# Four column tiles for every dense product, scores that ride along, a compact head layout and a residual on GpSimd, in a two-layer attention and MLP kernel

## Chip, cores, metric

One core of one Trainium2 chip. The metric is the device time of one execution in microseconds (us), median of the runs named; lower is better. Ratios are the mean time of one kernel's fast runs over that of the other's fast runs of the same rounds, so they are not quite the ratio of the medians quoted.

## The reference

Twice in turn: multi-query attention (32 heads of 16, one shared key and value head) and a mixer with an MLP, each on a normalised input, each with a residual. 2048 tokens of 512 features, bf16.

```python
def _A_ref(x, wq, wk, wv, wo):
    q = (x @ wq).reshape(B, S, 32, 16).transpose(0, 2, 1, 3)
    k, v = x @ wk, x @ wv
    p = softmax(einsum("bhqd,bkd->bhqk", q, k) * 16 ** -0.5)
    return einsum("bhqk,bkd->bhqd", p, v)...reshape(B, S, 512) @ wo

def _B_ref(x, w1, w2, w3, w4):
    h = gelu(layernorm(x) @ w1)          # then four quarters shifted by 1, -1, 2, -2 tokens
    x1 = x + shifted(h) @ w2
    return x1 + gelu(layernorm(x1) @ w3) @ w4      # w3: 512 x 1792

x = x + _A(layernorm(x)); x = x + _B(layernorm(x))     # and once more with the same weights
```

## The kernel before

The file contains a greedy planner. Each piece of work is declared with an engine, a priority, what it reads and writes, and a guess of its duration; the planner plays the engines forward in time, takes the best ready piece for each, and then writes out one fixed order for each engine with semaphore waits. Nothing is decided at run time. The order on TensorE distinguishes three shapes of the array: "Q" for scores (four row tiles of 32 rows), "P" for value products (four column tiles of 32 columns) and "F" for full 128 x 128 products. A product of another shape costs a switch.

The work is cut into half-blocks: two heads, 512 queries, 128 keys, 2048 of them in all. Most go to ScalarE (one exponential over 1024 columns); the others go to VectorE as a "pair", which makes exp from integer steps in four instructions.

```python
def declare_unit(self, g):                       # a half-block on ScalarE: two scores, one exponential
    q = op("PE", fpe, ..., pe=("Q", 512, 256, hs), prio=0)
    op("ACT", lambda e: e.activation(self.EA[...], self.PB[:, b0:b0 + 2, :], ACTF.Exp, scale=0.25),
       dur=0.0505 + 1024 / 1200, prio=0)
    ...
def declare_pair(self, g):                       # a half-block on VectorE
    for i in range(2):
        L = Late()                               # takes one of three spare PSUM banks
        op("PE", ..., pe=("Q", 512, 128, (h,)), prio=0.5, take=L)
        op("DVE", lambda e: e.tensor_scalar(out=J[...], in0=self.PB[:, L.bank, :], ...), give=L)
    for k in (1, 2):                             # two shifted copies
        op("DVE", lambda e: e.tensor_scalar(out=self.JK[:, r, :], in0=J, scalar1=float(self.STEPS[k]),
                                            scalar2=None, op0=ALU.add), dur=t_x4(1024), prio=2)
    ...                                          # one value product each for J, JK, JK
def outproj(self, la, tb, prio=4):               # a dense product: full shape
    ... e.matmul(self.PB[:, L.bank, :], lhsT=self.OT[:, b, q:q + 128], rhs=self.WO[:, b, :], ...)
    op("PE", fpe, ..., pe=mm(512, 2))            # mm() says shape "F"
```

`mlp` does the two wide products with W3 and W4 and adds the residual as a ninth product with the identity. A head's 16 rows stand in 32 partitions, half of them zero, so the query and output projections compute twice what they need. Where the planner's own count of TensorE's activity runs short it adds a "filler", a product with zero weights.

The softmax here doesn't subtract the row's maximum and nothing guards it: scores larger than these inputs give would overflow.

Of the kernel before, what the change touches and what calls it, by code (L numbers as in the profile page):

```python
# [26 lines left out]
class Op:  # L27
    __slots__ = ("eng", "emit", "preds", "npend", "succ", "dur", "prio", "seq", "ready", "start",
                 "end", "take", "give", "dma", "out", "pos", "sem", "vc", "side", "placed", "pe", "feeds")


class Plan:
# [7 lines left out]
    DRAIN = {"ACT": 0.15, "DVE": 0.085, "POOL": 0.1}  # L40
    SELF = 0.035
    MARGIN = 0.2
# [5 lines left out]
    CREDIT = 0.3  # L48
    URGENT = 0.4
    FORCE = 0.6  # L50
    CAP = 1.0
    WAITING = 12.0
    BUNCH = 2
    ALONE = 11
    PATIENCE = 3.0
    SLACK = 0
    NEAR_FILL = 0.2

    def __init__(self, nc, pool_banks):
        self.nc = nc  # L60
        self.res = {}
        self.ops = []
        self.now = 0.0
        self.free_at = {e: 0.0 for e in ENGINES}
        self.heap = {e: [] for e in ENGINES}
        self.order = {e: [] for e in ENGINES}
        self.events = [0.0]
        self.pool = [(0.0, b) for b in pool_banks]
        self.pool_last = {}
        self.left = 0  # L70
        self.dma_free = 0.0
        self.pe_kind = None
        self.pe_end = 0.0
        self.lane = [0.0] * 4
        self.window = 0
        self.activity = [0.0]
        self.warm = False
        self.release = 0.0
        self.pace = None
        self.filler = None  # L80
        self.debt = 0.0
        self.debt_at = 0.0
        self.base = 10.0
        self.units = []

    def op(self, eng, emit, reads=(), writes=(), dur=0.1, prio=None, take=None, give=None,
           dma=0, out=False, side=True, pe=None):
# [3 lines left out]
        o.pe = pe  # L91
        o.feeds = None
# [28 lines left out]
        if self.pace is not None and side:  # L121
            if pe is not None:
                self.release += pe[1] * self.pace / 2400.0
            o.ready = max(o.ready, self.release)
# [51 lines left out]
    def _pick(self, eng, t, dense=False):  # L176
# [6 lines left out]
        pressing = joins and any(o.prio == 0 and o.ready <= t + 1e-9 for o in h) and self.pe_kind != "Q"  # L183
        best = None
        bank = None
        for o in h:
# [11 lines left out]
            key = (low.get(o, o.prio), o.seq)  # L198
            if best is not None and key > best[0]:
                continue  # L200
# [65 lines left out]

    def lend(self, banks, o):
# [9 lines left out]
    def _place(self, o, t):  # L277
# [5 lines left out]
        if o.dma:  # L283
            s = max(t + 1.6, self.dma_free)
            o.end = s + o.dma / 330e3 + 0.6
            self.dma_free = s + o.dma / 330e3
            self.free_at[o.eng] = t + 0.06
# [21 lines left out]
        else:  # L309
            self.free_at[o.eng] = t + o.dur  # L310
            o.end = t + o.dur + self.DRAIN[o.eng]
        heapq.heappush(self.events, self.free_at[o.eng])
        if o.give is not None:
# [3 lines left out]
            heapq.heappush(self.events, o.end + self.MARGIN)  # L317
        for s in o.succ:
# [42 lines left out]
    def emit(self):  # L361
# [6 lines left out]
        nd = 0  # L368
        for o in todo:
            kn = known[o.eng]  # L370
            cand = []
# [19 lines left out]
            if o.dma:  # L391
                nd += 1
                key = f"d{nd}"
                sems[key] = nc.alloc_semaphore(key)
                o.sem = (key, 16)
# [13 lines left out]
        def body(eng):  # L409
            def f(e):  # L410
                for waits, emit, sem, inc in code[eng]:
                    for k, v in waits:
                        e.wait_ge(sems[k], v)
                    emit(e).then_inc(sem, inc)
# [28 lines left out]

EPS = 1e-5
# [3 lines left out]
class Kernel:  # L448
# [13 lines left out]
    STEPS = (0, 43, 85)  # L462
    PARTS = (0.3203125, 0.25390625, 0.2021484375)
# [3 lines left out]
    AHEAD = 7  # L467
    MAX_PAIRS = 2
    BACKLOG = 4
# [24 lines left out]
    def memory(self):  # L494
# [13 lines left out]
        self.WO = sb("WO", [8, 512])  # L508
# [8 lines left out]
        self.OT = sb("OT", [8, 512])  # L517
# [14 lines left out]
        self.SM = sb("SM", [5, 16], dt.float32)  # L532
# [12 lines left out]
        self.SPILL += [(qt[:, i * 512:(i + 1) * 512], [("QT", p, 2 * i), ("QT", p, 2 * i + 1)]) for i in range(4)]  # L545

# [20 lines left out]
    def build(self):  # L567
        with contextlib.ExitStack() as self.stack:
# [3 lines left out]
            self.pl.filler = self.filler if self.FILL else None  # L572
            self.pl.run(self.pump)
            self.pl.emit()

    def head(self):
# [42 lines left out]
        for j in range(3):  # L619
            fill("POOL", self.VD[:, j, :, :, 16:17], self.PARTS[j], vd, 0.2, -7)  # L620
        for c in range(4):
# [3 lines left out]
            if c == 0:  # L625
                self.qproj(0, 0, prio=-6, blocks=(0,))
            if c == 2:
                self.qproj(0, 0, prio=-5, blocks=range(1, 8))
# [5 lines left out]
        fill("POOL", self.WO, 0.0, [("WO",)], 3.5, 3)  # L634
        fill("POOL", self.GP[:, 0, :, 0:2], 0.0, [("GPL", 0)], 0.1, 3)
        wo4 = ins["A_wo"].rearrange("(b g d) n -> g d b n", b=8, g=4, d=16)
        for g in range(4):
            load(self.WO[32 * g:32 * g + 16, :, :], wo4[g], [("WO",)], 131072, 5)
# [15 lines left out]
    def rstd(self, tiles, prio, both=False):  # L654
# [4 lines left out]
        s0, s1, s2, s3, s4 = (self.SM[:, i, a:b] for i in range(5))  # L659
# [10 lines left out]
        root(s0, mv, s4, tg("MV"), tg("R1"), tg("S4"))  # L670
        if both:
# [4 lines left out]
            root(s3, s2, s4, tg("S2"), tg("R2"), tg("S4"))  # L676

# [24 lines left out]
    def ln_in(self, la, tiles, prio=None):  # L702
# [6 lines left out]
        for tb in tiles:  # L709
            op("DVE", lambda e, tb=tb: e.tensor_scalar(  # L710
                out=self.ZR[:, tb % 4, :], in0=src(tb), scalar1=self.MV[:, tb, 0:1],
                scalar2=self.SM[:, 0, tb:tb + 1], op0=ALU.subtract, op1=ALU.mult),
               reads=[("X", tb), ("MV", tb), ("R1", tb)], writes=[("ZR", tb % 4)], dur=0.456 if la else 0.355, prio=prio)
# [51 lines left out]
    def qproj(self, la, c, prio=None, blocks=range(8)):  # L765
# [7 lines left out]
        for b in blocks:  # L773
# [18 lines left out]
    def make_groups(self):  # L792
# [34 lines left out]
        self.di = 0  # L827
# [10 lines left out]
        self.pairs = []  # L838
        self.fin_left = {}
# [17 lines left out]
    def filler(self):  # L857
# [5 lines left out]
        if self.main_done or dep is not None and not (dep.placed and dep.end + self.pl.MARGIN <= self.pl.now):  # L863
            if not any(t + self.pl.MARGIN <= self.pl.now for t, b in self.pl.pool):
# [3 lines left out]
            "PE", lambda e: e.matmul(self.PB[:, self.ACC if L is None else L.bank, :], lhsT=self.NIL,  # L868
                                     rhs=self.ONES, start=L is not None, stop=L is not None, skip_group_check=True),
            reads=[("ONES",), ("ACC0",)], pe=mm(512), prio=-20, take=L, give=L)  # L870
# [30 lines left out]
    def declare_pair(self, g):  # L901
# [20 lines left out]
        for k in (1, 2):  # L922
            r = (2 * m + k - 1) % self.N_JK
            o = op("DVE", lambda e, k=k, r=r: e.tensor_scalar(  # L924
                out=self.JK[:, r, :], in0=J, scalar1=float(self.STEPS[k]), scalar2=None, op0=ALU.add),
               reads=jt, writes=[("JK", r)], dur=t_x4(1024), prio=2, side=False)
# [47 lines left out]
    def block_end(self, la, c, b, end):  # L974
# [40 lines left out]
        for h in range(nq // 2):  # L1015
# [10 lines left out]
        op("DVE", lambda e: e.tensor_tensor(out=self.OT[:, b, 0:n], in0=acc, in1=self.PB[:, M.bank, 0:n],  # L1026
                                            op=ALU.mult),
           reads=[("ACCF", m)], writes=[M, ("OT", b)], dur=t_ps(n), prio=5, give=M)
        if end == "add" and b >= 3:
            self.qproj(1, 1, prio=11, blocks=(2 * b - 6, 2 * b - 5))  # L1030
            if b == self.SPILLED - 1:
                self.qproj(1, 1, prio=11, blocks=range(2 * b - 4, 8))
# [5 lines left out]
    def pump(self, now):  # L1038
# [13 lines left out]
        if self.assign(now):  # L1052
# [10 lines left out]
    def assign(self, now):  # L1063
# [6 lines left out]
        d = max(self.di, self.hi + self.AHEAD)  # L1070
        while d < len(self.halves) and (self.halves[d][7] or self.halves[d][5] != self.ndve % 2):
            d += 1
        if d >= len(self.halves):
# [6 lines left out]
        self.di = d + 1  # L1080
        self.given.add(d)
        self.declare_pair(g)
# [3 lines left out]
    def chunk_end(self, la, c):  # L1086
# [11 lines left out]
        elif la == 0 and not (self.SPILLED > 3 and m == 1):  # L1098
            self.qproj(1, m, prio=11)
# [16 lines left out]
    def outproj(self, la, tb, prio=4):  # L1116
# [3 lines left out]
        for h in range(4):  # L1120
            def fpe(e, h=h):
                ins = None
                for b in (2 * h, 2 * h + 1):
                    ins = e.matmul(self.PB[:, L.bank, :], lhsT=self.OT[:, b, q:q + 128], rhs=self.WO[:, b, :],  # L1124
                                   start=(b == 0), stop=(b == 7))
                return ins
            op("PE", fpe, reads=[("OT", b) for b in range(8)] + [("WO",)], writes=[L], pe=mm(512, 2),
# [6 lines left out]
    def mixer_in(self, la, c, tiles, tail):  # L1134
# [3 lines left out]
        for tb in tiles:  # L1138
            op("DVE", lambda e, tb=tb: e.tensor_scalar(
                out=self.Y[:, tb % 6, :], in0=self.X32[:, tb, :], scalar1=self.MV[:, tb, 0:1],  # L1140
                scalar2=self.SM[:, 0, tb:tb + 1], op0=ALU.subtract, op1=ALU.mult),
               reads=[("X", tb), ("MV", tb), ("R1", tb)], writes=[("Y", tb % 6)], dur=0.456)
            op("DVE", lambda e, tb=tb: e.tensor_scalar(
                out=self.ZR[:, tb % 4, :], in0=self.Y[:, tb % 6, :], scalar1=self.SM[:, 3, tb:tb + 1],
                scalar2=None, op0=ALU.mult),
               reads=[("Y", tb % 6), ("R2", tb)], writes=[("ZR", tb % 4)], dur=0.265)
# [6 lines left out]
        for f in range(4):  # L1153
            L = Late()
            for h in range(2):
                def fpe(e, f=f, h=h, L=L):
                    ins = None
                    for dc in (2 * h, 2 * h + 1):
                        ins = e.matmul(self.PB[:, L.bank, 0:n], lhsT=self.W1[:, dc, f * 128:(f + 1) * 128],  # L1159
                                       rhs=ZT[:, dc, 0:n], start=(dc == 0), stop=(dc == 3))  # L1160
                    return ins
                op("PE", fpe, reads=zt + [("W1",)], writes=[L], pe=mm(n, 2),
# [29 lines left out]
    def mix(self, la, tb):  # L1192
# [5 lines left out]
        for h in range(2):  # L1198
            def fpe(e, h=h):
                ins = None  # L1200
                for f in (2 * h, 2 * h + 1):
                    a = t0 - self.SHIFTS[f]
                    ins = e.matmul(self.PB[:, L.bank, :], lhsT=self.GP[:, par, f, a:a + 128],  # L1203
                                   rhs=self.W2[:, f, :], start=(f == 0), stop=(f == 3))
# [6 lines left out]
            op("PE", fpe, reads=rd, writes=[L], pe=mm(512, 2), take=L if h == 0 else None)  # L1211
# [4 lines left out]
    def mlp(self, la, tiles, tail):  # L1216
# [4 lines left out]
        for tb in tiles:  # L1221
            op("DVE", lambda e, tb=tb: e.tensor_scalar(
                out=self.ZR[:, tb % 4, :], in0=self.Y[:, tb % 6, :], scalar1=self.MV[:, tb, 0:1],
                scalar2=self.SM[:, 0, tb:tb + 1], op0=ALU.subtract, op1=ALU.mult),
               reads=[("Y", tb % 6), ("MV", tb), ("R1", tb)], writes=[("ZR", tb % 4)], dur=0.325)
# [4 lines left out]
        for f in range(14):  # L1230
            L = Late()
            for h in range(2):
                def fpe(e, f=f, h=h, L=L):
                    ins = None
                    for dc in (2 * h, 2 * h + 1):
                        ins = e.matmul(self.PB[:, L.bank, 0:n], lhsT=self.W3[:, dc, f * 128:(f + 1) * 128],  # L1236
                                       rhs=ZT[:, dc, 0:n], start=(dc == 0), stop=(dc == 3))
                    return ins
                op("PE", fpe, reads=zt + [("W3",)], writes=[L], pe=mm(n, 2),
# [17 lines left out]
        for i, tb in enumerate(tiles):  # L1257
            L = Late()

            for h in range(8):  # L1260
                def fpe(e, h=h, i=i, tb=tb, L=L):
                    if h == 7:
# [56 lines left out]
```

## Time and profile before

| | before |
|---|---|
| time, median of 3 | 1708.66 us (1708.56 to 1714.65) |
| ScalarE, VectorE, TensorE busy | 91%, 82%, 98% of the span |
| half-blocks on ScalarE, on VectorE | 1558, 490 |
| ScalarE's idle time after its first exponential and before its last | 76 us, 50 of them between 700 and 1000 us |
| from the last exponential to the end | 87 us |

The first three rows are from the profile's first and fifth part; the prediction shows their lines. "The change of layers" means 700 to 1000 us: layer 1's attention can use only the keys whose tokens have gone through layer 0's MLP. "The tail" is the time after the last exponential.

### The profile page before, as it was taken

The page shows a single profiled execution, that of the slowest core. Times are in us where ns is not written, and L with a number is a line of the kernel's source. Part 1 is how long each engine was busy: PE and PEld are TensorE (multiplying, and loading weights), DVE is VectorE, ACT ScalarE, POOL GpSimd, SP SyncE. Part 2 cuts the span into 40 slices and gives each one's busy share as a digit, 9 for nine tenths or more (in the row PEclk, how much of TensorE's full clock was granted, in tenths as well). Part 3 has the DMA queues.
Part 4 walks back from the last instruction along what each step waited for, and adds up shares of the span by engine and source line. Part 5 has one row for each costly group of instructions (what it writes and reads, how often), then busy time and mean ns, then how long its engine had stood idle before and what let it go on. Part 6 is the DMA issues. An engine that isn't in the chain of part 4 may idle for free.

```text
span 1707.2 us, 37918 instructions
## 1 busy us (share of the span) xinstructions
PE 1672.0 (98%) x16522; PEld 555.0 (33%) x16522; DVE 1398.7 (82%) x2957; ACT 1545.6 (91%) x1632; POOL 62.6 (4%) x129
## 2 busy tenths in 40 slices
PE   8999999999999999999999999999999999999999
PEld 3322223323322222323223432223223224444444
DVE  8887999889998789898677568899889988668752
ACT  3999999999999999998978499999999999998912
POOL 2000000000000000000000000000000000000000
PEclk9999999999999999999999999999999999999999
DMA  5000000000000000000000000000000000000000
GB/s 186 2 1 1 1 1 1 1 1 1 2 2 1 1 1 1 2 1 1 1 1 1 1 1 2 2 1 2 5 4 4 2 1 2 8 8 2 2 13 16
DMA packets 10199, 12.42 MB, mean 7 GB/s; under 512 B 1584, under 2 KB 9520, under 8 KB 10032
## 3 DMA queue, kind: packets, MB, share of 16 engines
q1 hardware_dynamic: 10032, 10.00, 1.8%
q8 instruction: 129, 2.11, 0.5%
q14 instruction: 38, 0.31, 0.1%
HBM read 7.90 MB, written 2.10 MB: 6 GB/s over the span
## 4 chain that ended last, share of the span: by engine, by line
ACT 52%; PE 43%; DVE 4%; DMA 0%; issue 0%; POOL 0%; SPq 0%; POOLq 0%
ACT EA L895 48%; PE PB L851 14%; PE PB L966 11%; PE PB L1267 4%; PE PB L1236 4%; PE PB L868 3%; ACT G L1253 2%; PE PB L1124 2%; PE PB L1203 1%; PE PB L781 1%; ACT L895 1%; DVE J L916 1%; PE PB L690 1%; PE PB L1159 1%; DVE ST L649 1%; PE PB L1020 1%
## 5 line engine op out<-in xcount | busy, mean ns | idle before, releaser
L895 ACT ACTIVATE EA<-PB 128x1024 bf16<-128x1024 f32 x1558 | 1438.7, 1077 | 93.0 <-PE PB L851 56.6
L916 DVE TENSOR_SCALAR J<-PB 128x512 uint16<-128x512 f32 x980 | 634.4, 684 | 100.5 <-PE PB L851 95.5
L851 PE MATMUL PB<-QT,KT 32*128 32x512 bf16 (+1 forms) x4608 | 661.9, 359 | 14.4 <-ACT EA L895 9.9
L966 PE MATMUL PB<-EA,VP 128*32 128x512 bf16 (+1 forms) x3510 | 416.6, 360 | 1.0 <-DVE ACCF L994 0.3
L924 DVE TENSOR_SCALAR JK<-J 128x1024 uint16<-128x1024 uint16 x980 | 363.4, 420 | 37.7 <-PE PB L966 35.5
L851 PEld LDWEIGHTS PB<-QT,KT 32*128 32x128 bf16 x4608 | 172.2, 91 | 553.9 <-ACT EA L895 431.1
L966 PE MATMUL PB<-JK,VD 128*32 128x512 bf16 (+1 forms) x2196 | 256.9, 361 | 0.3 <-DVE JK L924 0.3
L966 PE MATMUL PB<-J,VD 128*32 128x512 bf16 (+1 forms) x1098 | 158.9, 362 | 0.4 <-DVE J L916 0.2
L966 PEld LDWEIGHTS PB<-EA,VP 128*32 128x32 bf16 x3510 | 111.7, 94 | 129.6 <-issue 107.2
L868 PE MATMUL PB<-ONES,NIL 128*128 128x512 bf16 x421 | 135.8, 394 | 11.5 <-DVE ST L649 2.5
L1236 PE MATMUL PB<-ZT,W 128*128 128x384 bf16 (+2 forms) x560 | 125.4, 339 | 0.4 <-DVE X L1130 0.3
L1267 PE MATMUL PB<-W,G 128*128 128x512 bf16 x448 | 121.4, 382 | 1.7 <-ACT G L1253 1.5
L966 PEld LDWEIGHTS PB<-JK,VD 128*32 128x32 bf16 x2196 | 71.4, 95 | 91.2 <-issue 47.9
L1246 DVE CAST G<-PB 128x512 bf16<-128x512 f32 (+2 forms) x126 | 73.2, 583 | 21.1 <-PE PB L1236 18.7
L781 PE MATMUL PB<-YT,WQ 128*32 128x512 bf16 (+1 forms) x1152 | 77.0, 359 | 0.1
L1124 PE MATMUL PB<-WO,OT 128*128 128x512 bf16 x256 | 74.1, 383 | 0.0
L868 PEld LDWEIGHTS PB<-ONES,NIL 128*128 128x128 bf16 x421 | 36.1, 98 | 86.6 <-issue 23.3
L1253 ACT ACTIVATE G<-G 128x3584 bf16<-128x3584 bf16 (+2 forms) x18 | 46.0, 2601 | 18.2 <-DVE G L1246 18.1
L666 POOL TENSOR_SCALAR SM<-MV 128x4 f32<-128x4 f32 (+3 forms) x30 | 8.9, 295 | 1363.7 <-DVE MV L651 1363.7
L1236 PEld LDWEIGHTS PB<-ZT,W 128*128 128x128 bf16 x560 | 41.4, 97 | 48.9 <-issue 26.3
L1026 DVE TENSOR_TENSOR OT<-ACCF,PB 128x512 bf16<-128x512 bf16 (+1 forms) x72 | 44.7, 622 | 11.6 <-PE PB L1020 11.2
L966 PEld LDWEIGHTS PB<-J,VD 128*32 128x32 bf16 x1098 | 43.2, 94 | 30.3 <-issue 22.2
(83 smaller groups left out, 850.2 us busy)
## 6 DMA issues: line engine op xcount, KB each, us to landing
W<-in_B_w_dram SPq DMA_DIRECT2D x2, 1792.0 KB, 12.3
X<-in_A_x_dram SPq DMA_DIRECT2D x8, 256.0 KB, 6.4
out_dram<-OUTB SPq DMA_DIRECT2D x16, 128.0 KB, 1.7
W<-in_B_w_dram SPq DMA_DIRECT2D x2, 512.0 KB, 6.5
WQ<-in_A_wq_dram SPq DMA_DIRECT2D x1, 512.0 KB, 5.8
WO<-in_A_wo_dram SPq DMA_DIRECT2D x4, 128.0 KB, 3.2
WK<-in_A_wk_dram SPq DMA_DIRECT2D x1, 16.0 KB, 6.0
WV<-in_A_wv_dram SPq DMA_DIRECT2D x1, 16.0 KB, 6.0
```

The costliest lines, as they stand in the source:

```text
L781: ins = e.matmul(self.PB[32 * g:32 * g + 32, L.bank, 0:n], lhsT=self.WQ[:, dc, w0:w0 + 32], rhs=self.YT[:, slot, dc, n0:n0 + n], start=(dc ...
L851: ins = e.matmul(self.PB[:, bank, j * n:(j + 1) * n], lhsT=self.KT[32 * h:32 * h + 32, la, (kb + j) * 128:(kb + j + 1) * 128], rhs=self.QT ...
L868: "PE", lambda e: e.matmul(self.PB[:, self.ACC if L is None else L.bank, :], lhsT=self.NIL, rhs=self.ONES, start=L is not None, stop=L is ...
L895: o = q.feeds = op("ACT", lambda e: e.activation(self.EA[:, ea, :, :], self.PB[:, b0:b0 + 2, :], ACTF.Exp, scale=0.25), writes=bk + [("EA" ...
L916: o = op("DVE", lambda e, i=i, L=L: e.tensor_scalar(out=J[:, i * 512:(i + 1) * 512], in0=self.PB[:, L.bank, :], scalar1=128 * LOG2E * 0.25 ...
L924: o = op("DVE", lambda e, k=k, r=r: e.tensor_scalar(out=self.JK[:, r, :], in0=J, scalar1=float(self.STEPS[k]), scalar2=None, op0=ALU.add), ...
L966: ins = e.matmul(self.PB[32 * h:32 * h + 32, self.ACC, 0:w], lhsT=v[:, la, kb + j, :], rhs=ap[:, i, j * w:(j + 1) * w], start=first and j ...
L1124: ins = e.matmul(self.PB[:, L.bank, :], lhsT=self.OT[:, b, q:q + 128], rhs=self.WO[:, b, :], start=(b == 0), stop=(b == 7))
L1236: ins = e.matmul(self.PB[:, L.bank, 0:n], lhsT=self.W3[:, dc, f * 128:(f + 1) * 128], rhs=ZT[:, dc, 0:n], start=(dc == 0), stop=(dc == 3))
L1246: op("DVE", lambda e, f=f, L=L: e.tensor_copy(self.G2[:, f, 0:n], self.PB[:, L.bank, 0:n]), writes=[L, ("G2", f)], dur=t_ps(n), give=L)
L1253: ins = e.activation(self.G2[:, a:a + 7, 0:n], self.G2[:, a:a + 7, 0:n], ACTF.Gelu_apprx_tanh)
L1267: ins = e.matmul(self.PB[:, L.bank, :], lhsT=self.G2[:, f, i * 128:(i + 1) * 128], rhs=self.W4[:, f, :], start=(f == 0), stop=False)
```

## The change

Its intent: TensorE is nearly full, so take work and shape switches off it. (1) Every dense product becomes four products in 32-column tiles, the value products' shape. (2) VectorE's scores are chosen at the moment a ScalarE score is placed, in the two row tiles that are free, so that they ride along. (3) The padded half of the query and output projections is dropped; the rows are spread by DMA. (4) GpSimd adds the residual in place of the identity product. (5) Constants of the planner are tuned again. Besides, each JK instruction (VectorE's shifted copies) gets a second operation, a multiplication by 1.0. The core of the diff:

```diff
+    def dot(self, e, bank, n, lhsT, rhs, start, stop):
+        for g in range(4):
+            ins = e.matmul(self.PB[32 * g:32 * g + 32, bank, 0:n], lhsT=lhsT[:, 32 * g:32 * g + 32], rhs=rhs,
+                           start=start, stop=stop, tile_position=(0, 32 * g), skip_group_check=True)
...
-            op("PE", fpe, reads=..., writes=[L], pe=mm(512, 2), ...)
+            op("PE", fpe, reads=..., writes=[L], pe=tiled(512, 2), ...)          # (1), in all dense products
...
+    def attach(self, q):                                                         # (2), called when a score is placed
+        if sum(1 for t, b in self.pl.pool if t + 0.06 <= self.pl.now) >= self.FREE:
+            self.assign(self.pl.now, 1 - q.pe[3][0] // 2)
-        if self.assign(now):
+        if now > self.attached + self.LONELY and self.assign(now, self.ndve % 2):
-    AHEAD = 7
+    AHEAD = 2
+    FREE = 2
+    LONELY = 4
...
-        self.WO = sb("WO", [8, 512])                                             # (3)
+        self.WO = sb("WO", [4, 512])
+        op("SP", lambda e: [
+            e.dma_start(self.OT[r0 + 16 * h:r0 + 16 * h + 16, b // 2, 0:n], self.OS[32 * h:32 * h + 16, m, 0:n])
+            for h in range(4)], reads=[("OS", m)], writes=[("OT", b)], dma=128 * n, parts=4, prio=5)
...
+            op("POOL", lambda e, tb=tb: e.tensor_tensor(out=self.X32[:, tb, :], in0=self.Y[:, tb % 6, :],   # (4)
+                                                       in1=self.X32[:, tb, :], op=ALU.add), ...)
-            for h in range(8):
+            for h in range(7):
-                    if h == 7:
-                        return e.matmul(self.PB[:, L.bank, :], lhsT=self.IDENT, rhs=self.Y[:, tb % 6, :], ...)
...
-    MARGIN = 0.2                                                                 # (5), and others
+    MARGIN = 0.15
-    PATIENCE = 3.0
+    PATIENCE = 2.0
```

## The prediction

> **What bounds the kernel now.** I read the page's first two parts, then the costliest groups, then the busy time by stage, then the waits, then the order of the matmuls.
>
> ```profile
> PE 1672.0 (98%) x16522; PEld 555.0 (33%) x16522; DVE 1398.7 (82%) x2957; ACT 1545.6 (91%) x1632; POOL 62.6 (4%) x129
> ...
> L895 ACT ACTIVATE EA<-PB 128x1024 bf16<-128x1024 f32 x1558 | 1438.7, 1077 | 93.0 <-PE PB L851 56.6
> L916 DVE TENSOR_SCALAR J<-PB 128x512 uint16<-128x512 f32 x980 | 634.4, 684 | 100.5 <-PE PB L851 95.5
> ...
> L924 DVE TENSOR_SCALAR JK<-J 128x1024 uint16<-128x1024 uint16 x980 | 363.4, 420 | 37.7 <-PE PB L966 35.5
> ...
> L868 PE MATMUL PB<-ONES,NIL 128*128 128x512 bf16 x421 | 135.8, 394 | 11.5 <-DVE ST L649 2.5
> ```
>
> The 2048 half-blocks of scores (two heads, 1024 columns) are shared out: 1558 get their exponential on ScalarE, the other 490 on VectorE (four instructions each). One half-block costs ScalarE 1438.7 / 1558 = 0.923 us, and VectorE (634.4 + 363.4) / 490 = 2.04 us. VectorE's other 401 us are evictions and norms. The 421 products with NIL only keep TensorE's clock up.
>
> The busy times by stage (columns: stretch, its length, then PE, PEld, DVE, ACT, POOL busy):
>
> ```profile
> 50.00:700.00 650.00, 645.52 (x6139) 192.12 (x6133) 573.69 (x1202) 645.98 (x689) 15.96 (x31) 1.00 0.01 1
> 700.00:1000.00 300.00, 288.40 (x2313) 94.74 (x2311) 223.24 (x468) 249.96 (x255) 12.10 (x25) 1.00 0.00 1
> 1000.00:1400.00 400.00, 396.77 (x3927) 119.38 (x3924) 351.84 (x732) 399.46 (x427) 9.18 (x19) 1.00 0.01 2
> 1400.00:1640.00 240.00, 234.59 (x3273) 98.02 (x3272) 182.76 (x397) 215.65 (x221) 10.13 (x22) 1.00 0.02 5
> 1640.00:1707.00 67.00, 61.90 (x349) 31.86 (x347) 25.42 (x57) 12.29 (x21) 2.70 (x8) 1.00 0.05 17
> ```
>
> From 50 to 700 and from 1000 to 1400 us ScalarE never stops (over 99%), while VectorE is at 88%: **ScalarE bounds over 60% of the run, and only moving half-blocks to VectorE helps there.** From 700 to 1000 (the change of layers) ScalarE idles 50 us, from 1400 to 1640 24 us. The last 67 us are a serial tail. The waits say who holds the engines up:
>
> ```profile
> DVE J L916 <- PE PB L851: 95.5, 123, 9.1
> ACT EA L895 <- PE PB L851: 56.6, 21, 17.6
> ACT EA L895 <- PE PB L966: 35.4, 20, 6.3
> ```
>
> VectorE waits 95.5 us for its scores, ScalarE 56.6 + 35.4 for TensorE. So TensorE is the second bound. What fills its 98%? Three consecutive matmul groups between 506 and 507 us show it (start, length):
>
> ```profile
> 506.17 0.39 PE L966 MATMUL PB<-EA,VP 128*32 128x512 bf16 x2
> 506.49 0.39 PE L868 MATMUL PB<-ONES,NIL 128*128 128x512 bf16 x1
> 506.81 0.39 PE L851 MATMUL PB<-QT,KT 32*128 32x512 bf16 x2
> ```
>
> Value products (128*32), full products (128*128) and scores (32*128) are three shapes of the array. Starts are 0.32 us apart, though 512 columns stream in 0.216 (next fence): each change of shape costs about 0.105 us. Taking all matmuls in order of start I count 3404 changes, 357 us, beside 1279 us of streaming: 1636 of 1707 us.
>
> **What the Trainium skill says.**
> 1. "TensorEngine Tiling (Array Packing)", Tiling Modes, Key Properties: changing the tiling mode drains TensorE, and tiles work independently. The 0.105 us above agrees. Its Restrictions add that column tiling gives up the fast weight load; no harm from that shows in the trace, where weight loads are hidden in either shape.
> 2. "VectorE: DVE Perf Modes", Mode 4×_2P: four slices do op0 and four op1, so a second operation with a constant is free. This matters because the JK step gets a multiplication by 1.0. The JK step's 420 ns for 1024 elements is the four-a-cycle rate (an estimate with that page's 0.96 GHz: 267 ns plus its fixed 150 cycles), so 420 should stay.
> 3. "GPSIMD Engine Reference", Elementwise: an add of 2048 elements takes 4497 ns, so 512 take about 1.1 us (an estimate). The same page has GpSimd share an SBUF interface with VectorE. The kernel before shows no such add.
> 4. "DMA: Bandwidth & Descriptors", Anatomy of one DMA: about 2.0 us fixed. The output stores here land 1.7 us after issue, which agrees.
>
> **The change part by part.**
>
> *Four column tiles for dense products.* The same columns stream, with four times the instructions. The query projection already has this form, so its rate can be read:
>
> ```profile
> 29.88 2.34 PE L781 MATMUL PB<-YT,WQ 128*32 128x512 bf16 x40
> 1697.61 3.19 PE L1267 MATMUL PB<-W,G 128*128 128x512 bf16 x14
> ```
>
> Ten sets of four: (2.34 − 0.38) / 9 = 0.218 us a set; full products: (3.19 − 0.38) / 13 = 0.216. At 256 columns sets of four come at about 0.109 to 0.117 against 0.109. Tiling itself thus costs and gains nothing; its gain is in shape changes. At least two per ScalarE half-block stay (scores, then something else): 2 × 1558 = 3116 of 3404. At most 288 × 0.105 = 30 us of TensorE.
>
> *Query projection without padded columns*: 64 groups of four products become half as many, except the first two and the eight of layer 1's second chunk. By the chunk table 46 groups of 512 columns become 23 and 16 of 256 become 8. TensorE loses 23 × 4 × 0.216 + 8 × 4 × 0.109 = 23 us, and VectorE 23 evictions of 0.684 and 8 of 0.41 us: 19 us. In exchange the rows are spread by DMA (groups of four, late by some 4 us), at low priority and long before use.
>
> *Output projection*: 256 full products become 128 sets: 128 × 0.216 = 28 us less. Each block's result now goes through four DMAs; about 4 us late (an estimate: 1.7 us landing plus issue), which counts only where a chunk's last block holds up what follows: the change of layers and the tail.
>
> *Residual on GpSimd*: 32 identity products leave TensorE, 7 us. 32 adds of about 1.1 us arrive on an engine that is 4% busy, before they are needed. They may hold up VectorE's two-port steps now and then: 32 × about 0.5 = at most 16 us of VectorE, probably half.
>
> *Scores ride along*: VectorE's scores are now chosen at the moment a ScalarE score is placed, in the other two row tiles. Scores stream 390 us in my count; 1558 ScalarE half-blocks need 1558 × 0.216 = 337. So most ride already and only about 53 us of TensorE is left to gain. The larger effect is that VectorE gets scores on time: part of the 95.5 us.
>
> *Sum.* TensorE is relieved of 30 + 23 + 28 + 7 + 53 = some 140 us, 8% of its load, and stops being a second bound. Then VectorE, not TensorE, decides how many half-blocks leave ScalarE. I let VectorE rise from 88% to 94% between 50 and 700 and 1000 and 1400: 0.06 × 1050 / 2.04 = 31 more. The evictions saved give 19 / 2.04 = 9. In 1400 to 1640 VectorE rises from 76% to 84%: another 9. That is 49 half-blocks, 49 × 0.923 = **45 us** off ScalarE, and off the end, because ScalarE is the bound there. At the change of layers TensorE is what ScalarE waits for; of 50 us idle I take 10 back, the last wait of 12.9 us being a serial chain. In the tail 7 identity products (1.5 us) and half an output projection (2 us) go, and the 4 us of DMA come: nothing. GpSimd's hold on VectorE returns 2. 1708.7 − 45 − 10 + 2 = **1655 us**.
>
> **The rivals.**
> *A: VectorE's idle time is not the score wait.* It also lacks PSUM: three spare banks serve pairs and all dense work, and a pair needs two free at the moment of riding. Then it stays near 490 half-blocks, and only the change of layers and the evictions count: 1708.7 − 10 − 9 = about 1690. For it: 95.5 us is only a third of VectorE's 308 us idle. Against: pairs were held back by TensorE's occupancy, which falls.
> *B: full balance.* VectorE reaches 95% everywhere: 70 to 80 more half-blocks, 65 to 74 us, with 20 at the change of layers: about 1620. For it: a planner that had been tuned again. Against: VectorE's dense work comes in clumps.
> *C: the new waits cost more than is saved*: the DMAs and GpSimd's adds stand in the chain between the layers and in the tail, 5 to 10 us each time, and VectorE loses 16 us: about 1710. Against: priorities put the residual early, and blocks of other work cover most DMAs.
>
> **Range and chances.** 1655 with A and B as the sides: 1612 to 1694. Faster by over 2% means under 1674.5, that is at least about 20 half-blocks moved with the 10 us at the change of layers: 0.73. Rival A and weaker forms of it lie within 2%: 0.23. Rival C going badly: 0.04.
>
> **What would show it.** The exponentials on ScalarE at about 1509, at 0.923 us each; VectorE's J and JK at about 1078 each with 684 and 420 ns (a JK of 500 or more would refute step 2); VectorE at 87 to 90% of the span; the wait of J for L851's matmuls well under 95 us; full 128*128 products left only for transposes, values and sums; fewer changes of shape, about 3100; the idle of ScalarE between 700 and 1000 about 40 us. The prediction is wrong if ScalarE's count stays near 1558, or if it falls and ScalarE idles instead.

## The result

1643.45 us, median of 4 runs (1643.41 to 1644.47), against 1709.0 for the kernel before: ratio 0.961, 95% interval 0.959 to 0.963. That is 65.6 us less, where 54 were predicted. The first part and the costliest groups of the changed kernel (EA is ScalarE's exponential; J and JK are VectorE's four instructions for a half-block):

```profile
PE 1617.8 (99%) x21141; PEld 545.5 (33%) x21141; DVE 1414.8 (86%) x2978; ACT 1535.7 (94%) x1623; POOL 105.6 (6%) x162
...
L997 ACT ACTIVATE EA<-PB 128x1024 bf16<-128x1024 f32 x1545 | 1423.2, 1084 | 58.4 <-PE PB L1075 34.1
L1018 DVE TENSOR_SCALAR J<-PB 128x512 uint16<-128x512 f32 x1006 | 651.0, 683 | 107.5 <-PE PB L953 103.4
...
L1028 DVE TENSOR_SCALAR JK<-J 128x1024 uint16<-128x1024 uint16 x1006 | 387.5, 427 | 13.6 <-PE PB L1075 7.6
```

The exponentials fell from 1558 to 1545, by 13, not by the 49 predicted. VectorE waits as long for its scores as before, 103.4 us against 95.5. ScalarE's busy time fell by 10 us (1545.6 to 1535.7), so some 56 of the 65.6 us are time in which ScalarE did nothing, in the run or after its last exponential. Busy time by stage (stretch, length, then PE, PEld, DVE, ACT, POOL):

```profile
50.00:700.00 650.00, 645.34 (x7414) 191.41 (x7406) 584.71 (x1207) 649.48 (x693) 29.60 (x43) 1.00 0.04 8
700.00:1000.00 300.00, 295.06 (x3816) 100.40 (x3814) 255.29 (x546) 270.96 (x281) 18.42 (x29) 1.00 0.02 4
1000.00:1400.00 400.00, 395.90 (x4884) 121.33 (x4876) 350.19 (x720) 399.64 (x422) 19.23 (x26) 1.00 0.03 8
1400.00:1576.00 176.00, 175.08 (x3196) 78.96 (x3192) 155.71 (x342) 175.51 (x182) 15.91 (x27) 1.00 0.04 9
```

From 50 to 700 us ScalarE was already full. The steady stretches are no faster at all: counting the exponentials plus half of the J instructions, from 50 to 700 us the kernel before finishes 675 + 454 / 2 = 902 half-blocks and the changed one 676 + 456 / 2 = 904. In the 400 us from 1000 it is 551 and 541. The change of layers is where they differ, and the groups of that stretch say so (before, then after):

```profile
L895 ACT ACTIVATE EA<-PB 128x1024 bf16<-128x1024 f32 x237 | 220.2, 1062 | 49.8 <-PE PB L851 25.2 <-PE PB L966 24.5
L916 DVE TENSOR_SCALAR J<-PB 128x512 uint16<-128x512 f32 x129 | 82.9, 684 | 23.7 <-PE PB L851 23.0
```
```profile
L997 ACT ACTIVATE EA<-PB 128x1024 bf16<-128x1024 f32 x266 | 245.9, 1074 | 28.8 <-PE PB L1075 28.8
L1018 DVE TENSOR_SCALAR J<-PB 128x512 uint16<-128x512 f32 x166 | 107.5, 682 | 23.3 <-PE PB L953 22.7
```

301.5 half-blocks before, 349 after: 47.5 more in the same 300 us, at a steady 1.39 a us (902 in 650) worth 34 us. The rest is in the tail. What TensorE still does after the last exponential (the costliest groups from 1620 to 1707 us before, and from 1582 to 1642 us after):

```profile
L1267 PE MATMUL PB<-W,G 128*128 128x512 bf16 x126 | 28.7, 379 | 0.2 <-ACT G L1242 0.2
L868 PE MATMUL PB<-ONES,NIL 128*128 128x512 bf16 x68 | 19.9, 383 | 3.2 <-DVE MV L651 1.1 <-DVE ZR L1222 0.8 <-DVE ST L649 0.3
```
```profile
L607 PE MATMUL PB<-W,G 128*32 128x512 bf16 x330 | 18.7, 379 | 0.2 <-ACT G L1353 0.2
L607 PE MATMUL PB<-ZT,W 128*32 128x256 bf16 (+1 forms) x512 | 17.5, 296 | 0.0
L607 PE MATMUL PB<-ONES,NIL 128*32 128x512 bf16 x180 | 13.6, 383 | 1.4 <-DVE ST L713 0.4 <-DVE OUTB L1388 0.4 <-DVE MV L715 0.2
```

Of the products with W4 (PB<-W,G) 126 were left over for the tail, now 330 / 4 = 82.5. Dense work that had fallen behind the attention is now done beside it. The whole balance, each row from the traces:

| us | before | after | difference |
|---|---|---|---|
| before the first exponential | 19.6 | 19.6 | 0 |
| ScalarE busy from first to last exponential | 1524.5 | 1521.4 | -3 |
| ScalarE idle in the head, up to 60 us | 9.5 | 6.2 | -3 |
| idle at the change of layers | 50.0 | 29.0 | -21 |
| idle elsewhere | 16.5 | 6.3 | -10 |
| tail | 87.0 | 59.0 | -28 |
| span | 1707.2 | 1641.6 | -66 |

TensorE, laid end to end in order of start: each product counts for the time that no earlier one covers, at the planner's 2.4 columns a ns (the measured 0.216 us for 512 columns are 2.37). In us:

| streaming | before | after |
|---|---|---|
| scores | 390 | 355 |
| value products | 389 | 450 |
| dense products | 389 | 342 |
| fillers | 90 | 80 |
| transposes | 21 | 21 |
| changes of shape | 3404, 346 us | 3264, 332 us |

### The profile page after: what moved, and what is told of

It is laid out like the page before. It is cut to its first block, busy times and chain, and to the rows that moved or that the text cites. A ratio compares the mean times of both kernels' runs of the same rounds, so it can differ in the third digit from the quotient of the medians.

```text
span 1641.6 us, 47631 instructions
## 1 busy us (share of the span) xinstructions
PE 1617.8 (99%) x21141; PEld 545.5 (33%) x21141; DVE 1414.8 (86%) x2978; ACT 1535.7 (94%) x1623; POOL 105.6 (6%) x162
## 4 chain that ended last, share of the span: by engine, by line
ACT 75%; PE 22%; DVE 2%; DMA 0%; POOL 0%; issue 0%; SPq 0%; POOLq 0%
ACT EA L997 70%; PE PB L607 10%; PE PB L953 6%; PE PB L1075 5%; ACT G L1364 2%; ACT L997 1%; ACT GP L1288 1%; ACT L1288 1%; PE PB L773 1%; ACT L1364 0%; DVE ST L713 0%; DVE G L1357 0%; DVE ZR L756 0%; DMA X<-in_A_x_dram 0%; POOL X L1371 0%; DVE J L1018 0%
## 5 line engine op out<-in xcount | busy, mean ns | idle before, releaser
L1018 DVE TENSOR_SCALAR J<-PB 128x512 uint16<-128x512 f32 x1006 | 651.0, 683 | 107.5 <-PE PB L953 103.4
L953 PE MATMUL PB<-QT,KT 32*128 32x512 bf16 (+1 forms) x4608 | 623.3, 360 | 9.9 <-ACT EA L997 7.1
L1075 PE MATMUL PB<-EA,VP 128*32 128x512 bf16 (+1 forms) x3482 | 465.6, 362 | 0.9 <-DVE ACCF L1107 0.3
L1075 PE MATMUL PB<-JK,VD 128*32 128x512 bf16 (+1 forms) x2252 | 331.8, 361 | 0.2
L607 PE MATMUL PB<-ZT,W 128*32 128x512 bf16 (+2 forms) x2816 | 170.8, 344 | 0.5 <-DVE J L1018 0.4
L607 PE MATMUL PB<-ONES,NIL 128*32 128x512 bf16 x1416 | 143.7, 392 | 4.5 <-DVE ZR L756 1.3
L607 PE MATMUL PB<-W,G 128*32 128x512 bf16 x1792 | 125.2, 382 | 0.3 <-ACT G L1353 0.2
L607 PEld LDWEIGHTS PB<-ZT,W 128*32 128x32 bf16 x2816 | 57.4, 96 | 56.0 <-issue 33.4
L1135 DVE TENSOR_TENSOR OS<-ACCF,PB 128x512 bf16<-128x512 bf16 (+1 forms) x72 | 44.7, 621 | 12.6 <-PE PB L1129 8.1
L607 PEld LDWEIGHTS PB<-W,G 128*32 128x32 bf16 x1792 | 37.5, 95 | 46.9 <-issue 26.8
L1371 POOL TENSOR_TENSOR X<-Y,X 128x512 f32<-128x512 bf16 x32 | 38.4, 1204 | 154.4 <-DVE Y L1326 149.6
```

The lines of the kernel that those rows point to most:

```text
L607: ins = e.matmul(self.PB[32 * g:32 * g + 32, bank, 0:n], lhsT=lhsT[:, 32 * g:32 * g + 32], rhs=rhs, start=start, stop=stop, tile_position= ...
L953: ins = e.matmul(self.PB[:, bank, j * n:(j + 1) * n], lhsT=self.KT[32 * h:32 * h + 32, la, (kb + j) * 128:(kb + j + 1) * 128], rhs=self.QT ...
L1018: o = op("DVE", lambda e, i=i, L=L: e.tensor_scalar(out=J[:, i * 512:(i + 1) * 512], in0=self.PB[:, L.bank, :], scalar1=128 * LOG2E * 0.25 ...
L1075: ins = e.matmul(self.PB[32 * h:32 * h + 32, self.ACC, 0:w], lhsT=v[:, la, kb + j, :], rhs=ap[:, i, j * w:(j + 1) * w], start=first and j ...
L1135: op("DVE", lambda e: e.tensor_tensor(out=self.OS[:, m, 0:n], in0=acc, in1=self.PB[:, M.bank, 0:n], op=ALU.mult), reads=[("ACCF", m)], wri ...
L1371: op("POOL", lambda e, tb=tb: e.tensor_tensor(out=self.X32[:, tb, :], in0=self.Y[:, tb % 6, :], in1=self.X32[:, tb, :], op=ALU.add), reads ...
```

## The experiments

Three theories. **Theory 1**, the prediction's: ScalarE is the bound; time falls with the half-blocks moved to VectorE. **Theory 2**: over the whole run TensorE's throughput is the bound. Its priorities feed ScalarE first, so what it lacks shows as dense work left for the change of layers and the tail. **Theory 3** (in one run): VectorE holds things back.

One thing had to be settled first. The planner is greedy, and a tiny change of a guess reorders everything after it. The planner prints nothing, but it holds its own forecast of the end. I let it plan every variant twelve times with one guessed duration shifted in steps of 0.5 ns, from 0.063 to 0.0685 us (a "draw"). For the kernel before the forecasts run from 1686 to 1717, median 1697, and its own is 1696. For the changed kernel they run from 1616 to 1669, median 1636, and **its own is the lowest of the twelve**. So each variant below is the draw with the forecast nearest to its median, and is to be compared with the *redraw* of the changed kernel (e1), not with the changed kernel. The forecasts are guesses of a planner, not times; over the thirteen kernels below that use its unaltered durations the chip took 13 to 29 us more.

| run | what | forecast | chip, median of 4 | half-blocks on VectorE |
|---|---|---|---|---|
| before | | 1696 | 1709 | 490 |
| after | | 1616 | 1643.5 | 503 |
| e1 | changed, redrawn | 1636 | 1661.7 | 503 |
| e2 | changed, no riding | 1670 | 1691.5 | 492 |
| e3 | changed, full products | 1644 | 1664.5 | 498 |
| e4 | changed, more on VectorE | 1666 | 1681.4 | 553 |
| e5 | before, half of the wide products | 1628 | 1651.2 | 494 |
| e6 | changed, one shifted copy | 1615 | 1638.1 | 525 |
| e7 | before, tiles alone | 1688 | 1703.6 | 493 |
| e8 | before, riding alone | 1680 | 1697.2 | 497 |
| e9 | changed, residual on TensorE | 1648 | 1671.1 | 509 |
| e10 | changed, padded heads | 1666 | 1694.5 | 497 |
| e11 | changed, planned again | 1631 | 1645.1 | 525 |
| e12 | compact heads alone | 1674 | 1697.9 | 497 |

All were timed in three rounds.

**The clock.** Runs differ in the clock granted to TensorE, and the time goes with it: the kernel before took 1707.7 to 1709.3 us at 0.999 to 1.000 and 1713.1 to 1714.6 at 0.996; e2 took 1685.8 at 0.995 and 1701.0 at 0.983. That is about 1.3 us for each 0.001. The changed kernel and e1 were profiled at 1.000, but e4 (0.995 to 0.996), e10 and e12 (0.994 to 0.996), e6 (0.991 to 0.993), e5 (0.993 to 0.999) and e2 (0.983 to 0.995) never ran there. Where it matters the difference at like clock is added; e1 took 1666.0 us at 0.996.

**e1, the order alone.**

```diff
-    return 0.066 + n * 1.043e-3
+    return 0.063 + n * 1.043e-3
```

> The changed kernel with one planning constant 3 ns smaller (the planner's guess of a VectorE eviction, 0.063 us in place of 0.066); no instruction's work changes, only the order that the greedy planner falls into. The planner's own forecast of the end over twelve such draws runs from 1616 to 1669 with a median of 1636; the changed kernel is the lowest, 1616, and measured 1643; this draw forecasts 1636. Theory 'the parts of the change are the whole gain': within 0.3% of the changed kernel, about 1643. Theory 'some of the gain is a picked order': about 1660, that is 15 to 20 us slower, with the same 503 or so half-blocks on VectorE and the loss as idle time of ScalarE at the change of layers and in the tail.

1661.65 us, ratio to before 0.972. The same work in another order (fillers aside) costs 18 us. ScalarE has the same 1545 exponentials; the tail is 82.5 us (59.0 in the changed kernel) and the idle time at the change of layers 38.1 (29.0). So 18 of the 65.6 us are the picked order, and 47.5 are what the parts give in a middling order.

**e4, the predicted step**: more half-blocks for VectorE, which may now go after 1 us without waiting for a ride.

```diff
-    LONELY = 4
+    LONELY = 1
```

> The changed kernel with one number changed: a pair for VectorE may be assigned without a ride after 1 us in place of 4. A median draw; the plan then gives VectorE 553 half-blocks, 50 more. This is the step of my prediction done by itself. Theory 1 (predicted): 50 x 0.923 = 46 us less on ScalarE, and so about 40 us off the redraw: 1615 to 1625. Theory 2: ScalarE's busy time does fall by 46 us, but VectorE and TensorE then leave more dense work for the change of layers and the tail, ScalarE idles more than it saved, and the time is above the redraw by 10 to 40 us: 1670 to 1700.

1681.37 us, 20 us slower than e1 (15 at like clock). The exponentials fell to 1495, and ScalarE's busy time from first to last exponential from 1508.6 to 1460.3 us: the 46 us that the arithmetic promised are there. But idle time at the change of layers rose from 38.1 to 82.9 and the tail from 82.5 to 95.2. The stages of e4:

```profile
50.00:700.00 650.00, 640.99 (x7092) 192.48 (x7092) 618.73 (x1309) 648.82 (x694) 22.03 (x35) 1.00 0.03 7
700.00:1000.00 300.00, 286.02 (x3936) 106.21 (x3932) 234.13 (x502) 217.06 (x220) 23.81 (x38) 0.99 0.02 4
```

VectorE reaches 95% up to 700 us (618.73 of 650), as I had hoped for. Then, at the change of layers, ScalarE works 217 of 300 us. Theory 1's 40 us less didn't come. TensorE shows what did: from 50 to 700 us it streams 76 us of dense products against 95 in e1, at the change of layers 90 against 74, and after the last exponential 64 against 56. Dense work was pushed back, and layer 1's keys come out of that work. The run is not the predicted step alone, though: half-blocks taken without a ride leave scores unpaired (396 us of scores in all against 355 in e1), so part of what displaced the dense work is TensorE's time for scores. In e11 below, 22 more half-blocks, with 367 us of scores, gained nothing either.

**e5, TensorE relieved and nothing else** (the kernel before; the result is wrong by construction).

```diff
-                    for dc in (2 * h, 2 * h + 1):        # W3
+                    for dc in (2 * h,):
-                    for f in (2 * h, 2 * h + 1):         # W4
+                    for f in (2 * h,):
```

> Wrong result on purpose. The kernel before with only every second product of the two wide layers (W3 and W4): some 97 us of TensorE streaming less (half of 224 x 0.216 + 224 x 0.162 + 112 x 0.109 and of 448 x 0.216), nothing less on ScalarE or VectorE. A median draw. Theory 1 (ScalarE bounds; TensorE only at the change of layers): 10 to 20 us less than the kernel before, about 1692. Theory 2 (TensorE's throughput bounds through the dense work that is left over): 55 to 80 us less, 1630 to 1655, with ScalarE's busy time unchanged within 10 us and nearly all of the gain in the tail and the idle time at the change of layers.

1651.17 us, 58 us less than the kernel before (63 at like clock), for 97 us of streaming taken away: 0.6 us a us. Exponentials 1554 against 1558. The stage of the change of layers:

```profile
700.00:1000.00 300.00, 290.50 (x2462) 88.52 (x2458) 240.43 (x521) 285.49 (x294) 11.96 (x24) 0.98 0.00 1
```

ScalarE is busy for 285 us where the kernel before had 250, and the tail is 47.3 us instead of 87.0. That is theory 2's forecast, in place and size. Part of the tail needs no catching up, as what is left over is itself half as long: products with W3 and W4 stream 45 us in the tail of the kernel before, half of that is 22.5, and e5 has 15.

**e6, VectorE relieved and nothing else** (wrong result on purpose, relative error 0.020).

```diff
-        for k in (1, 2):
+        for k in (1,):
...
+        es.append(es[-1])
```

> Wrong result on purpose. The changed kernel in which a pair makes one shifted copy (JK) in place of two and the value product reads it twice: some 500 x 0.385 = 190 us of VectorE less at equal pairs, nothing less on TensorE. A median draw; the plan takes only 525 half-blocks on VectorE. Theory 3 (VectorE is what keeps dense work and pairs back): 60 us or more off the redraw, under 1600. Theory 2 (TensorE bounds): 10 to 25 us off the redraw, about 1640, though twice as much engine time is removed as from TensorE in the run with half of the wide products.

1638.08 us, 23.6 us less than e1, and an estimated 33 at like clock (9 us for the missing 0.007). VectorE's busy time fell by 120 us (1414.6 to 1294.7), so a us of VectorE is worth 0.2 to 0.3, less than half of a us of TensorE. It took only 22 more half-blocks, and waited longer for scores than ever:

```profile
L1018 DVE TENSOR_SCALAR J<-PB 128x512 uint16<-128x512 f32 x1050 | 678.8, 684 | 179.8 <-PE PB L953 175.5
```

VectorE isn't the bound; theory 3, which asked for 60 us or more, falls.

**e2 and e8, the riding**, undone in the changed kernel and done alone in the kernel before (AHEAD and FAR went with it).

```diff
-            self.pl.attach = self.attach
-        if now > self.attached + self.LONELY and self.assign(now, self.ndve % 2):
+        if self.assign(now, self.ndve % 2):
-    AHEAD = 2
+    AHEAD = 7
```

> The changed kernel with the riding undone: VectorE's pairs are assigned as in the kernel before, whenever the conditions allow, seven half-blocks ahead. A median draw of twelve. Theory 1 (ScalarE bounds, as predicted): the gain comes from half-blocks moved, so with 492 of them on VectorE in place of 503 the time should be about 10 us over a redraw of the changed kernel, some 1665 to 1670. Theory 2 (TensorE's throughput bounds and dense work falls behind): scores that do not ride take TensorE 30 to 50 us more, and that shows as a longer tail and more idle time of ScalarE at the change of layers: about 1690 to 1700, with the busy time of ScalarE nearly unchanged.

> The kernel before with riding alone: VectorE's pairs are taken at the moment a ScalarE score is placed, with two banks free and in the other two row tiles. A median draw. Undoing it in the changed kernel cost 30 us. Theory 2: 12 to 30 us less than the kernel before, 1680 to 1697, with the streaming of scores down by some 35 us (390 to 355) and about the same number of half-blocks on VectorE (497). Theory 1: no more than 6 us, as only 7 half-blocks move.

e2: 1691.5 us (1685.8 to 1701.0), 24 to 39 us slower than e1; its scatter goes with TensorE's clock, 0.983 to 0.995 in its four runs, and at like clock it is some 20 us slower. e8: 1697.2 us, 12 us faster than the kernel before. Riding is one of the two largest parts. But my reason for it isn't confirmed. In e8 scores stream 31 us less than in the kernel before (391 to 360) and value products 38 us more (389 to 427); in e2 against e1 it is the reverse, +39 and -36. TensorE's sum hardly moves. What does change is what VectorE gets at the change of layers (e1, then e2):

```profile
L1018 DVE TENSOR_SCALAR J<-PB 128x512 uint16<-128x512 f32 x164 | 106.2, 683 | 19.6 <-PE PB L953 18.7
```
```profile
L1018 DVE TENSOR_SCALAR J<-PB 128x512 uint16<-128x512 f32 x127 | 82.0, 683 | 12.0 <-PE PB L953 11.5
```

18 half-blocks fewer there, while both have about 450 J instructions from 50 to 700 us (451 and 442). The trace of e2 is of its slowest run, at a clock of 0.97 in both stretches; but e8, at full clock, has 148 J instructions at the change of layers where the kernel before has 129. Whether that comes from riding, or from looking 2 instead of 7 half-blocks ahead when few keys are ready, these runs don't separate.

**e10 and e12, the compact heads**, undone in the changed kernel and, in e12, kept alone.

```diff
-    def qproj(self, la, c, prio=None, blocks=range(8), direct=False):
+    def qproj(self, la, c, prio=None, blocks=range(8), direct=True):
-        self.WO = sb("WO", [4, 512])
+        self.WO = sb("WO", [8, 512])
-        op("SP", lambda e: [e.dma_start(self.OT[...], self.OS[...]) for h in range(4)], ...)
```

> The changed kernel with the compact head layout undone: the query projection writes its padded layout directly, the attention output stays padded, the output projection takes eight contractions again; no scatter by DMA. A median draw. TensorE gets 23 + 28 = 51 us more, VectorE 19 us more. Theory 2 at 0.6 a us of TensorE, and VectorE at the 0.12 to 0.19 a us of the run with one shifted copy: 31 + 3 = about 34 us over the redraw, 1690 to 1700. Theory 1: VectorE's 19 us are 9 half-blocks, 8 us: 1670. If the DMAs cost time in the chain between the layers and in the tail, it would be less than either.

> The changed kernel with all undone but the compact head layout: full products, no riding, the residual on TensorE, the planner's older constants. A median draw. Theory 2 at 0.6 a us of TensorE: 51 us of TensorE and 19 of VectorE less than the kernel before give about 25 to 35 us less, 1675 to 1685. Theory 1: about 8 us less, 1700.

e10: 1694.5 us, 33 us over e1, where theory 2's rate gave 34. At like clock it is 28, and 4 of these lie before the first exponential (23.6 us in place of 19.6). Dense products stream 393 us there against 341 in e1, the 51 us counted. e12: 1697.9 us, only 12 us under the kernel before (17 at like clock), where I expected 25 to 35. Its tail is short (61.4 us) but ScalarE idles 56.0 us at the change of layers. Whether this part pays more beside the riding than alone isn't shown: 24 to 28 against 17 us is no more than the draws scatter.

**e3 and e7, the column tiles**, undone in the changed kernel and done alone.

```diff
-        for g in range(4):
-            ins = e.matmul(self.PB[32 * g:32 * g + 32, bank, 0:n], lhsT=lhsT[:, 32 * g:32 * g + 32], ...)
+        return e.matmul(self.PB[:, bank, 0:n], lhsT=lhsT, rhs=rhs, start=start, stop=stop, ...)
```

> The changed kernel with every dense product and filler as one 128 by 128 product again in place of four 32-column tiles; all else as changed. A median draw. Streaming time is the same (0.216 us for 512 columns either way), only changes of the array's shape come back: some 150 to 300 more at 0.105 us, 15 to 30 us of TensorE. Theory 1: hardly any effect, within 5 us of the redraw, because ScalarE bounds. Theory 2: 8 to 25 us slower than the redraw.

> The kernel before with every dense product and filler in four 32-column tiles and nothing else changed. A median draw. By the run with full products in the changed kernel (3 us) the tiles alone are worth 0 to 10 us: 1699 to 1709. If the tiles were what lets the rest work, they would give nothing alone and the same 3 us in the changed kernel; if they were the main part, 30 us or more.

e3: 1664.5 us, 3 us over e1. e7: 1703.6 us, 5 us under the kernel before (ratio 0.996, interval 0.993 to 0.998). The draws scatter more than that, so no effect beyond some 5 us is shown. Undoing the tiles brings the changes of shape from 3247 (e1) to 3490, 243 x 0.102 = 25 us of TensorE, but takes 12 us of dense streaming (341 to 329) and 5 of value products (448 to 443) away. Some 8 us are left, which at 0.6 a us fits the little that was measured; e7's tiles likewise add 11 us of dense streaming (389 to 400). So tiles have a price in short bursts: two dense products of 512 columns followed by a score take 548 ns from the first start to the score's as tiles (e1), 538 as full products (e3), by the median. Within a long burst they have none, as the tails show (before, then after):

```profile
1684.51 9.27 PE L1236 MATMUL PB<-ZT,W 128*128 128x384 bf16 x56
```
```profile
1619.35 9.27 PE L607 MATMUL PB<-ZT,W 128*32 128x384 bf16 x224
1629.22 6.23 PE L607 MATMUL PB<-W,G 128*32 128x512 bf16 x112 [0.16 <-ACT G L1353]
```

224 tile products of 384 columns take 9.27 us, exactly what 56 full ones took before; sets of four at 512 columns come every (6.23 - 0.38) / 27 = 0.217 us.

**e9, the residual back on TensorE.**

```diff
-            op("POOL", lambda e, tb=tb: e.tensor_tensor(out=self.X32[:, tb, :], in0=self.Y[:, tb % 6, :], ...))
-            for h in range(7):
+            for h in range(8):
+                    if h == 7:
+                        return self.dot(e, L.bank, 512, self.IDENT, self.Y[:, tb % 6, :], False, True)
```

> The changed kernel with the mixer's residual back on TensorE as an identity product (32 sets of four tiles, 7 us of streaming) and GpSimd's adds gone. A median draw. Theory 2 at the rate that the run with half of the wide products showed (58 us for 97 us of TensorE, 0.6 a us): 4 us over the redraw, 1666; the draws scatter more than that, so 1655 to 1675 says no more than that the part is small. A loss of 15 us or more would mean that the identity product stood in the tail's chain.

1671.1 us, 9.5 us over e1, the size of the draws' scatter; so the part is small, as expected. JK takes 418 to 420 ns in the six versions without GpSimd's 32 adds and 419 to 430 in the eight with them, so the adds hold up VectorE by at most about 1006 x 10 ns = 10 us.

**e11, a try at a better version.** Planned with the exponential at the 0.921 us that the traces show, and the best of 1740 draws of the constants.

```diff
-                         writes=bk + [("EA", ea)], dur=0.0505 + 1024 / 1200, prio=0, side=False)
+                         writes=bk + [("EA", ea)], dur=0.0675 + 1024 / 1200, prio=0, side=False)
```

> A try at a better version. The changed kernel planned with ScalarE's exponential at 0.921 us, as both traces show it, in place of 0.904, and the best forecast of 1740 draws of the planner's constants (525 half-blocks on VectorE, the first stretch of layer 1's keys 8 tiles long). The corrected planner forecasts 1631. Since its ScalarE time now agrees with the trace, the measured time should lie within 10 us of that, 1631 to 1645, that is 0 to 12 us under the changed kernel. If forecasts picked as the best of many are mostly luck that the chip doesn't share, it lands at 1650 to 1665.

1645.1 us, ratio to before 0.962: the same as the changed kernel, with 22 more half-blocks on VectorE and 10.8 us more tail (69.8). It is no better, and shows again that the number of half-blocks isn't what counts. No version here beats the changed kernel.

## Why the prediction was right or wrong

The time came out inside the range, 11.5 us below the middle, and that is luck: a term that failed was made up for by terms that had been put too low or at nothing. **The mechanism was wrong for most of it.** The prediction named its own test: it is wrong "if ScalarE's count stays near 1558". The count is 1545.

- *"49 half-blocks, 49 x 0.923 = 45 us off ScalarE, and off the end"*: this step failed. 13 moved. And where 50 were moved, in e4, the kernel became 20 us slower, not 46 faster (with fewer rides, as said above). The flaw was to read ScalarE's 99% in the steady stretches as the bound of the run. Those stretches borrow: TensorE serves ScalarE first and leaves dense work, which comes due at the change of layers and in the tail.
- *"Of 50 us idle I take 10 back"*: the mechanism was right and the size off, 21 us.
- *"In the tail ... nothing"*: wrong, 28 us. I priced only the work that left the tail, 1.5 and 2 us, and not the 43 products with W4 and others that now run before the last exponential. A further 10 us of idle time elsewhere I did not price at all.
- *TensorE relieved of 140 us*: dense products lost 47 of 58 us (the missing 11 are the tiles' price, as in e7), scores 35 of 53, and the shape changes fell by 140, not 288. Value products took 61 us more, which I had not foreseen. Yet the conclusion that relief of TensorE matters was the right one, for the wrong clients: not VectorE's scores but the dense work.
- *VectorE's wait for scores well under 95 us*: 103.4. Rival A, "VectorE's idle time is not the score wait", was right in this: VectorE stayed near 490. It was wrong to add only 10 us at the change of layers.
- *JK at 420, GpSimd's add at 1.1 us, DMA about 2 us*: 427 ns, 1.20 us and 1.8 us. These held. The multiplication in JK costs nothing: e9 has it without the adds, at 420 ns as before. The skill's 2.0 us is for DMAs that GpSimd issues, and those here are SyncE's, so the agreement is one of size. The equal rate of tiles held in long bursts only.
- *"At least about 20 half-blocks"* for 2% was a slip: 1708.7 - 1674.5 - 10 = 24 us are 26 half-blocks. "64 groups" of the query projection are 72 by the trace (1152 products in sixteens); the 23 and 8 that go are right.
- *The order itself* was in no term: 18 us of the gain, by e1, come from the one order that was picked. The median order would have given 1662, and the prediction would have been nearer still, for no better reason.

What stays open: theory 2's rate accounts for about half of what the parts gave. From the kernel before to e1, TensorE lost 25 us of streaming (fillers left out) and 157 x 0.102 = 16 us of shape changes; at 0.6 that is 25 of the 47.5 us. Open are therefore also how riding pays, 12 us alone and 20 to 30 in company, though TensorE's streaming doesn't fall, why value products pair less well, and how much of each part's number is its draw. Each part was measured in one draw, and the new constants of the planner (5) were never undone by themselves.

## What to carry to other kernels

An engine that is full in the long stretches isn't the bound if another one feeds it by postponing work: look at what is left over after the full engine's last instruction, and count work done per stretch, not busy shares. Before believing what a part of a change is worth in a kernel whose order comes from a greedy planner, redraw the order without changing any work; here that alone moved the time by 18 us. And test the promised step alone: moving 50 units off the "bound" engine made this kernel slower. And check what else the test's edit moves, and at what clock it ran.

## What the Trainium skill lacked or had wrong

- "TensorEngine Tiling (Array Packing)", Tiling Modes, says that changing the mode drains TensorE but gives no cost. In these traces a change between row tiles, column tiles and the full array costs about 0.10 us (346 us for 3404 changes in the kernel before).
- The same page's Restrictions list what column tiling gives up, without a cost. Here four column tiles streamed at the full array's rate in long bursts: 0.217 us a set against 0.216 at 512 columns, and 9.27 us for 56 sets of 384 columns either way. In bursts of two sets before a score they took 548 ns against 538.
- "GPSIMD Engine Reference", Elementwise, has only an fp32 add of 2048 elements. The add of 512 bf16 elements to fp32 took 1.20 us here, in line with it; VectorE's two-port step took 418 to 420 ns on average without these adds and 419 to 430 beside 32 of them.
- "DMA: Bandwidth & Descriptors", Anatomy of one DMA, has about 2.0 us fixed for the GpSimd path. Copies within SBUF of 16 KB issued by SyncE landed after 1.8 us, those of 64 KB after 2.4.
- "Trainium Kernel Development and Optimization" and the other pages read have no way of finding a bound that lies in postponed work: TensorE stood at 97 to 99% busy in every version here, from 1638 to 1709 us.
